# Chunked attention and a two-layer MLP: q and k transposed by VectorE in 32x32 blocks from the tenth group on

## Chip, cores and metric

The kernel runs on one core of a Trainium2 chip. The metric is the device time of one execution in microseconds (us). The engines are TensorE (PE in the profile; PEld is its weight load), VectorE (DVE), ScalarE (ACT), GpSimd (POOL, which also issues the loads) and SyncE (SP, which issues the stores).

## What is computed

```python
batch, n_heads, seq, head_dim = (8, 8, 576, 64)          # q, k, v, float32
# attention inside chunks of 64 positions
scores = (1 / sqrt(64)) * q_c @ k_c.T                     # per batch, head and chunk: 64 x 64
attn = exp(scores - max(scores)); attn = attn / (sum(attn) + 1e-9)
out = attn @ v_c
x = out.transpose(0, 2, 1, 3).reshape(4608, 512)          # tokens x (heads * head_dim)
# the MLP: d_model 512, d_ff 2048
h = x @ w_in
result = maximum(0.01 * h, h) @ w_out                     # 4608 x 512, float32
```

## The kernel before

All matrix work is in float16 with float32 sums. The 4608 tokens are cut into 36 groups of 128 tokens (two chunks of 64 positions); a batch of 576 tokens is 4.5 groups, so every second batch begins in the middle of a group. A group goes through a chain of stages, which the main loop interleaves: iteration `it` works on group `it` (transposes), `it - 1` (scores, softmax) and `it - 2` (attention output).

- `load_qk(u)` (L79): GpSimd issues one DMA for q and one for k of group u, with tokens on the partitions (128 tokens x 8 heads x 64), converted to float16 on the way; two DMAs each where the group straddles two batches. There are `NIN` = 9 buffers per tensor, and loads run five iterations ahead.
- `stage_t(u)`: eight TensorE transposes (L216 into `qp`, L218 into `kp`, with `ident`) put the head dimension on the partitions, two heads at a time. VectorE copies `qp` into the tile `QZ` in two halves of 64 partitions (L221), each into its own place between zeros; ScalarE copies `kp` to `KT` (L223).
- `stage_s(u)`: eight matmuls QZ x KT give the scores `Sp` of 8 heads and 2 chunks (L230). VectorE takes the maximum `mx` (L234) and subtracts it into `sh` (L236).
- `stage_x(u)`: ScalarE's exponential `ex` (L242).
- `stage_n(u)`: VectorE's sum `z` (L247), `ze`, reciprocal `zi`, and the product `en` (L253).
- `stage_e(u)`: four TensorE transposes of `en` into `tpe` (L261); VectorE copies them to `et` (L263).
- `stage_v(u)`: eight matmuls of `VB` (v of the batch) and `et` into `xp` (L272); ScalarE copies it to `xT` (L281), after which the group's 128 tokens may be used by the MLP. When a batch's last chunk is done, `load_v` (L92) issues the v of the batch after next into the same buffer, so its two DMAs wait on GpSimd's queue for those matmuls, and the q and k loads issued after them wait behind them.

The MLP is cut into 288 chunks of equal TensorE work. `mm1` (L151, 144 chunks) makes `hT` from `xT` and `w_inT`, and ScalarE takes the leaky relu into `gT` (L158). `mm2` (L167, 144 chunks, four to an output tile) makes `oP` from `gT` and `w_outT`; ScalarE copies a finished tile to `osb` (L176) and SyncE stores it. `fill(n)` issues the next n chunks of a fixed list, or stops when their tokens aren't there yet. Token blocks of the MLP are 128 (eight), 256 (two) and 512 (six) long.

Every engine executes its instructions in the order written. From iteration 5 on TensorE's order is: S of group it-1, `fill(2)`, E of it-2, T of it, `fill(2)`, V of it-2, `fill(2)`; VectorE's is mx, sh, et, the two copies to QZ, z, ze, zi, en. After the last group the chunks that are left are issued in one go.

Of the kernel before, what the change touches and what calls it, by code (L numbers as in the profile page):

```python
# [8 lines left out]
FP16 = mybir.dt.float16  # L9
# [7 lines left out]
def kernel(  # L17
# [21 lines left out]
    nc = tc.nc  # L39

    B, H, S, D = q.shape
# [3 lines left out]
    CH = 64  # L45
# [3 lines left out]
    SCL = float(D) ** -0.5  # L49
    NQZ = 3  # L50
    NVB = 2
    NIN = 9
    G = 2 * CH

    NU = n_tok // G
    BLOCKS = [128] * 8 + [256] * 2 + [512] * 6

    sbp = ctx.enter_context(tc.tile_pool(name="k_sb", bufs=1))
# [5 lines left out]
    QZ = [sbp.tile([128, 4, 2, 2, CH], FP16, name=f"QZ{i}") for i in range(NQZ)]  # L64
# [5 lines left out]
    def load_qk(u):  # L70

        both = []
        for name, src in (("q_in", q), ("k_in", k)):
            t = sbp.tile([128, H, D], FP16, name=name, tag=name, bufs=NIN)
            r0, r1 = u * G, (u + 1) * G
            cut = min(-(-r0 // S) * S, r1) if r0 % S else r1
            for a, z in ((r0, cut), (cut, r1)):
                if a < z:
                    nc.gpsimd.dma_start(  # L79
                        out=t[a - r0:z - r0],  # L80
                        in_=src[a // S, :, a % S:a % S + z - a, :].rearrange("h p d -> p h d"),
                    )
            both.append(t)
        qk[u] = tuple(both)

    def zero_vb(i, eng):
        for m in range(2):
            eng.memset(VB[i][m * CH:(m + 1) * CH, :, :, (1 - m) * CH:(2 - m) * CH], 0.0)

    def load_v(b):  # L90
        for m in range(2):
            nc.gpsimd.dma_start(  # L92
                out=VB[b % NVB][m * CH:(m + 1) * CH, :, :, m * CH:(m + 1) * CH].rearrange("p h c d -> p (h c) d"),
                in_=v[b, m * H // 2:(m + 1) * H // 2].rearrange("h (c j) d -> j (h c) d", j=CH),
            )
# [8 lines left out]
    def load_w_out(f0, f1):  # L104
# [3 lines left out]
        )  # L108

    load_qk(0)  # L110
    ident = sbp.tile([128, 128], FP16, name="ident")
    make_identity(nc, ident)
# [28 lines left out]
    def mm1(j, a):  # L141
        tb, r0 = BLOCKS[j], START[j]
        nf = 512 // tb
        if a == 0:
            tag, bufs, pad = ("gS", 4, 128) if tb == 128 else ("gT", 2, 512)
            gT[j] = sbp.tile([128, NFC, tb], FP16, name="gT", tag=tag, bufs=bufs, padded_shape=[128, NFC, pad])
        hT = psp.tile([128, nf, tb], FP32, name="hT", tag="mm", bufs=4)
        for i in range(nf):
            fc = nf * a + i
            for t in range(NT):  # L150
                nc.tensor.matmul(  # L151
                    out=hT[:, i, :],
                    lhsT=w_inT[:, t, fc * 128:(fc + 1) * 128],
                    rhs=xT[:, t, r0:r0 + tb],
                    start=(t == 0),
                    stop=(t == NT - 1),
                )
        nc.scalar.activation(  # L158
            out=gT[j][:, nf * a:nf * a + nf, :], in_=hT, func=AFT.Prelu, bias=0.0, scale=1.0, alpha=0.01
        )  # L160

    def mm2(j, ti, part):
        if part == 0:
            oP[j, ti] = psp.tile([128, d_model], FP32, name="oP", tag="mm", bufs=4)
        o = oP[j, ti]
        for fc in range(part * 4, part * 4 + 4):
            nc.tensor.matmul(  # L167
                out=o,
                lhsT=gT[j][:, fc, ti * 128:(ti + 1) * 128],
                rhs=w_outT[:, fc, :],  # L170
                start=(fc == 0),
                stop=(fc == NFC - 1),
            )
        if part == NFC // 4 - 1:
            osb = sbp.tile([128, d_model], FP32, name="osb", tag="osb", bufs=3)
            nc.scalar.activation(out=osb, in_=o, func=AFT.Copy, bias=0.0, scale=1.0)  # L176
            r0 = START[j] + ti * 128
            nc.sync.dma_start(out=out[r0:r0 + 128, :], in_=osb)
# [12 lines left out]
    def fill(n):  # L191
        for _ in range(n):
            if state["pos"] == len(chunks):
                return
            kind, j, a, p = chunks[state["pos"]]
            if START[j] + BLOCKS[j] > state["tokens"]:
                return
            state["pos"] += 1
            if kind == "mm1":
                mm1(j, a)  # L200
            else:
                mm2(j, a, p)
# [8 lines left out]
    def stage_t(u):  # L211
# [10 lines left out]
        KT[u] = sbp.tile([128, 4, 2, CH], FP16, name="KT", tag="KT", bufs=2)  # L222
        nc.scalar.activation(out=KT[u], in_=kp, func=AFT.Copy, bias=0.0, scale=1.0)  # L223

    def stage_s(u):
        qz, kt = QZ[u % NQZ], KT.pop(u)
        Sp = psp.tile([128, 8, CH], FP32, name="Sp", tag="Sp", bufs=1)
        for i in range(8):
            g, e, m = i // 4, i // 2 % 2, i % 2
            nc.tensor.matmul(  # L230
                out=Sp[:, i, :], lhsT=qz[:, 2 * m + g, e, :, :], rhs=kt[:, 2 * m + g, e, :], start=True, stop=True
            )
        mx = sbp.tile([128, 8], FP32, name="mx", tag="mx", bufs=2)
        nc.vector.tensor_reduce(out=mx, in_=Sp, axis=AXL.X, op=ALU.max)  # L234
        SH[u] = sbp.tile([128, 8, CH], FP32, name="sh", tag="sh", bufs=2)
        nc.vector.tensor_tensor(  # L236
            out=SH[u], in0=Sp, in1=mx.unsqueeze(2).to_broadcast((128, 8, CH)), op=ALU.subtract
        )

    def stage_x(u):  # L240
        E[u] = sbp.tile([128, 8, CH], FP16, name="ex", tag="ex", bufs=2)
        nc.scalar.activation(out=E[u], in_=SH.pop(u), func=AFT.Exp, bias=0.0, scale=SCL)  # L242

    def stage_n(u):
        ex = E.pop(u)
        z = sbp.tile([128, 8], FP32, name="z", tag="z", bufs=2)
        nc.vector.tensor_reduce(out=z, in_=ex, axis=AXL.X, op=ALU.add)  # L247
        ze = sbp.tile([128, 8], FP32, name="ze", tag="ze", bufs=2)
        nc.vector.tensor_scalar_add(out=ze, in0=z, scalar1=1e-9)
        zi = sbp.tile([128, 8], FP32, name="zi", tag="zi", bufs=2)  # L250
        nc.vector.reciprocal(out=zi, in_=ze)
        E[u] = sbp.tile([128, 8, CH], FP16, name="en", tag="en", bufs=2)
        nc.vector.tensor_tensor(  # L253
            out=E[u], in0=ex, in1=zi.unsqueeze(2).to_broadcast((128, 8, CH)), op=ALU.mult
        )

    def stage_e(u):
        en = E.pop(u)
        tpe = psp.tile([128, 4, 128], FP16, name="tpe", tag="ox", bufs=1)
        for i in range(4):  # L260
            nc.tensor.transpose(out=tpe[:, i, :], in_=en[:, 2 * i:2 * i + 2, :], identity=ident)  # L261
        et = sbp.tile([128, 2, 2, 2, CH], FP16, name="et", tag="et", bufs=2)
        nc.vector.tensor_copy(out=et, in_=tpe)  # L263
        ET[u] = et

    def stage_v(u):
        et = ET.pop(u)
        xp = psp.tile([128, NT, 2, CH], FP32, name="xp", tag="ox", bufs=1)
        for e in range(2):
            b, c = divmod(2 * u + e, NCH)  # L270
            for t in range(NT):
                nc.tensor.matmul(  # L272
                    out=xp[:, t, e, :],
                    lhsT=VB[b % NVB][:, t, c, :],
                    rhs=et[:, t // 2, e, t % 2, :],
                    start=True,
                    stop=True,
                )
            if c == NCH - 1 and b + NVB < B:
                load_v(b + NVB)  # L280
        nc.scalar.activation(out=xT[:, :, u * G:(u + 1) * G], in_=xp, func=AFT.Copy, bias=0.0, scale=1.0)  # L281
        state["tokens"] = (u + 1) * G


    for it in range(NU + 2):
        if it < 5:
            if it >= 2:
                stage_e(it - 2)
            if it >= 1:
                stage_s(it - 1)  # L290
            if it >= 2:
                stage_v(it - 2)
            if it >= 1:
                stage_x(it - 1)
            fill(2)
            if it >= 1:
                stage_n(it - 1)
            stage_t(it)
            if it > 2:
                fill(2)  # L300
        else:
            if it <= NU:
                stage_s(it - 1)
            fill(2)
            if it <= NU:
                stage_x(it - 1)
            stage_e(it - 2)
            if it < NU:
                stage_t(it)
            if it <= NU:  # L310
                stage_n(it - 1)
            fill(2)
            stage_v(it - 2)
            fill(2)
        if 0 < it and it + 5 < NU:
            load_qk(it + 5)
    fill(len(chunks))


# [28 lines left out]
```

## Time and profile before

| | us |
|---|---|
| median of 3 runs | 323.13 (322.86 to 324.0) |
| span of the profiled execution, first to last instruction | 322.2 |
| TensorE busy | 300.4 |
| ScalarE busy | 165.4 |
| VectorE busy | 161.5 |
| GpSimd busy, mostly issuing loads | 98.3 |

The page of the profile gives a span for the profiled execution and no other time of it; the times of the runs are of other executions. Busy shares are means over the span: the attention stages end at about 246 us, and from there on only the MLP is left.

### The profile page before, as it was taken

The page shows a single profiled execution, that of the slowest core. Times are in us where ns is not written, and L with a number is a line of the kernel's source. Part 1 is how long each engine was busy: PE and PEld are TensorE (multiplying, and loading weights), DVE is VectorE, ACT ScalarE, POOL GpSimd, SP SyncE. Part 2 cuts the span into 40 slices and gives each one's busy share as a digit, 9 for nine tenths or more (in the row PEclk, how much of TensorE's full clock was granted, in tenths as well). Part 3 has the DMA queues.
Part 4 walks back from the last instruction along what each step waited for, and adds up shares of the span by engine and source line. Part 5 has one row for each costly group of instructions (what it writes and reads, how often), then busy time and mean ns, then how long its engine had stood idle before and what let it go on. Part 6 is the DMA issues. An engine that isn't in the chain of part 4 may idle for free.

```text
span 322.2 us, 6197 instructions
## 1 busy us (share of the span) xinstructions
PE 300.4 (93%) x2608; PEld 182.8 (57%) x2608; DVE 161.5 (50%) x330; ACT 165.4 (51%) x290; POOL 98.3 (31%) x116
## 2 busy tenths in 40 slices
PE   2477789999999999999999999999999999999995
PEld 1367685578778677555555555555554444444442
DVE  5755757666766675777667667756760000000000
ACT  2244644456665565586348734883477137316611
POOL 8763997505800560490057036000000000000000
PEclk9997979999999999999999999999999999999999
DMA  9999999955990695499169429600100020020011
GB/s 69 175 193 187 182 154 149 196 68 67 174 99 33 46 181 45 88 154 66 65 72 167 33 41 184 79 2 36 65 34 2 35 96 2 2 96 35 0 65 65
DMA packets 121627, 28.18 MB, mean 87 GB/s; under 512 B 112896, under 2 KB 116992, under 8 KB 121600
## 3 DMA queue, kind: packets, MB, share of 16 engines
q0 software_dynamic: 116416, 18.36, 77.1%
q1 hardware_dynamic: 5184, 9.44, 7.9%
q8 instruction: 20, 0.33, 0.4%
q14 instruction: 7, 0.06, 0.0%
HBM read 36.70 MB, written 9.44 MB: 143 GB/s over the span
## 4 chain that ended last, share of the span: by engine, by line
PE 86%; DMA 9%; POOL 3%; issue 1%; ACT 1%; ACTq 0%; POOLq 0%
PE oP L167 39%; PE hT L151 36%; DMA w_outT<-in_moe_w_out_dram 4%; DMA k_in<-in_k_dram 3%; DMA w_inT<-in_moe_w_in_dram 3%; PE xp L272 2%; PE Sp L230 2%; PE tpe L261 2%; PE kp L218 2%; PE qp L216 2%; POOL k_in L79 1%; POOL VB L92 1%; POOL w_inT L99 1%; POOL q_in L79 0%; POOL w_outT L105 0%
## 5 line engine op out<-in xcount | busy, mean ns | idle before, releaser
L151 PE MATMUL hT<-xT,w_inT 128*128 128x128 f16 (+2 forms) x1024 | 139.0, 293 | 4.7 <-DMA w_inT<-in_moe_w_in_dram 3.0
L167 PE MATMUL oP<-w_outT,gT 128*128 128x512 f16 x576 | 132.7, 379 | 0.0
L158 ACT ACTIVATE gT<-hT 128x512 f16<-128x512 f32 x144 | 85.8, 597 | 42.9 <-PE hT L151 42.7
L151 PEld LDWEIGHTS <-w_inT 128*128 128x128 f16 x1024 | 80.9, 102 | 44.8 <-issue 5.2
L167 PEld LDWEIGHTS <-gT 128*128 128x128 f16 x576 | 53.4, 98 | 56.7
L176 ACT ACTIVATE osb<-oP 128x512 f32<-128x512 f32 x36 | 21.5, 597 | 75.0 <-PE oP L167 69.2
L234 DVE TENSOR_REDUCE mx<-Sp 128x8 f32<-128x512 f32 x36 | 24.9, 692 | 44.5 <-PE Sp L230 44.5
L92 POOL DMA_DIRECT2D VB<-in_v_dram x16 | 18.5, 1160 | 85.9 <-PE xp L272 85.9
L79 POOL DMA_DIRECT2D k_in<-in_k_dram x40 | 35.3, 882 | 7.2 <-DMA w_inT<-in_moe_w_in_dram 2.5
L79 POOL DMA_DIRECT2D q_in<-in_q_dram x40 | 35.3, 889 | 4.7 <-DMA w_outT<-in_moe_w_out_dram 1.8
L221 DVE COPY QZ<-qp 64x512 f16<-64x512 f16 x72 | 30.1, 418 | 5.1 <-PE qp L216 4.6
L242 ACT ACTIVATE ex<-sh 128x512 f16<-128x512 f32 x36 | 22.5, 624 | 11.6 <-DVE sh L236 11.6
L281 ACT ACTIVATE xT<-xp 128x512 f16<-128x512 f32 x36 | 21.4, 593 | 11.7 <-PE xp L272 11.7
L223 ACT ACTIVATE KT<-kp 128x512 f16<-128x512 f16 x36 | 21.3, 592 | 11.6 <-PE kp L218 11.6
L247 DVE TENSOR_REDUCE z<-ex 128x8 f32<-128x512 f16 x36 | 24.7, 686 | 4.4 <-ACT ex L242 3.4
L263 DVE COPY et<-tpe 128x512 f16<-128x512 f16 x36 | 15.3, 425 | 22.4 <-PE tpe L261 22.4
L253 DVE TENSOR_TENSOR en<-ex,zi 128x512 f16<-128x512 f16 x36 | 24.9, 691 | 1.2
L236 DVE TENSOR_TENSOR sh<-Sp,mx 128x512 f32<-128x512 f32 x36 | 24.9, 691 | 1.2
L216 PE MATMUL qp<-ident,q_in 128*128 128x128 f16 x144 | 14.9, 229 | 8.7 <-DMA q_in<-in_q_dram 8.7
L230 PEld LDWEIGHTS <-QZ 128*128 128x128 f16 x288 | 13.6, 100 | 9.1 <-DVE QZ L221 1.5
L272 PEld LDWEIGHTS <-VB 128*128 128x128 f16 x288 | 13.2, 99 | 6.6 <-issue 0.4
L230 PE MATMUL Sp<-KT,QZ 128*128 128x64 f16 x288 | 14.8, 196 | 2.2 <-ACT KT L223 1.3
(22 smaller groups left out, 108.9 us busy)
## 6 DMA issues: line engine op xcount, KB each, us to landing
out_dram<-osb SPq DMA_DIRECT2D x36, 256.0 KB, 2.0
VB<-in_v_dram POOLq DMA_DIRECT2D x16, 288.0 KB, 5.7
q_in<-in_q_dram POOLq DMA_DIRECT2D x32, 128.0 KB, 6.0
k_in<-in_k_dram POOLq DMA_DIRECT2D x32, 128.0 KB, 5.9
w_inT<-in_moe_w_in_dram POOLq DMA_DIRECT2D x8, 256.0 KB, 8.5
w_outT<-in_moe_w_out_dram POOLq DMA_DIRECT2D x4, 512.0 KB, 11.1
q_in<-in_q_dram POOLq DMA_DIRECT2D x8, 64.0 KB, 6.7
k_in<-in_k_dram POOLq DMA_DIRECT2D x8, 64.0 KB, 6.2
```

The lines of the kernel that those rows point to most:

```text
L79: nc.gpsimd.dma_start(out=t[a - r0:z - r0], in_=src[a // S, :, a % S:a % S + z - a, :].rearrange("h p d -> p h d"),)
L92: nc.gpsimd.dma_start(out=VB[b % NVB][m * CH:(m + 1) * CH, :, :, m * CH:(m + 1) * CH].rearrange("p h c d -> p (h c) d"), in_=v[b, m * H // ...
L151: nc.tensor.matmul(out=hT[:, i, :], lhsT=w_inT[:, t, fc * 128:(fc + 1) * 128], rhs=xT[:, t, r0:r0 + tb], start=(t == 0), stop=(t == NT - 1),)
L158: nc.scalar.activation(out=gT[j][:, nf * a:nf * a + nf, :], in_=hT, func=AFT.Prelu, bias=0.0, scale=1.0, alpha=0.01)
L167: nc.tensor.matmul(out=o, lhsT=gT[j][:, fc, ti * 128:(ti + 1) * 128], rhs=w_outT[:, fc, :], start=(fc == 0), stop=(fc == NFC - 1),)
L221: nc.vector.tensor_copy(out=qz[s * CH:(s + 1) * CH, :, :, s, :], in_=qp[s * CH:(s + 1) * CH])
L230: nc.tensor.matmul(out=Sp[:, i, :], lhsT=qz[:, 2 * m + g, e, :, :], rhs=kt[:, 2 * m + g, e, :], start=True, stop=True)
L234: nc.vector.tensor_reduce(out=mx, in_=Sp, axis=AXL.X, op=ALU.max)
L236: nc.vector.tensor_tensor(out=SH[u], in0=Sp, in1=mx.unsqueeze(2).to_broadcast((128, 8, CH)), op=ALU.subtract)
L242: nc.scalar.activation(out=E[u], in_=SH.pop(u), func=AFT.Exp, bias=0.0, scale=SCL)
L247: nc.vector.tensor_reduce(out=z, in_=ex, axis=AXL.X, op=ALU.add)
L253: nc.vector.tensor_tensor(out=E[u], in0=ex, in1=zi.unsqueeze(2).to_broadcast((128, 8, CH)), op=ALU.mult)
```

## The change

Groups 0 to 8 (batches 0 and 1) stay as they are. From group `UD` = 9 on:

- q and k come per batch, by `load_qk_batch(b)`, with 16 DMAs of GpSimd per batch: for each tensor, each half `m` of the heads, each pair of heads `s` and each half `dh` of the head dimension, one DMA to 32 partitions. A partition holds one position inside blocks of 32 positions; what is contiguous is 32 numbers of the head dimension (128 bytes read, 64 written). The tiles `q_d` and `k_d` have three buffers each. Batch b is issued at the end of iteration 9b // 2 - 5 (4, 8, 13, 17, 22, 26 for batches 2 to 7).
- VectorE's `transpose` turns each 32x32 block and writes QZ (`stage_dq`, two halves of 64 partitions x 512 elements) and KT (`stage_dk`, 128 x 512). A group that straddles two batches (13, 22 and 31) has each of them in two pieces, by `cuts`.
- The eight TensorE transposes and the three copies of `stage_t` are gone for these groups. VectorE's order becomes mx, sh, first half of q, et, second half of q, k, z, ze, zi, en.
- The heads pair up differently on the partitions, so `stage_v` reads `et` in another order.
- The last `fill(2)` of an iteration becomes `fill(3)` while such groups are prepared (iterations 9 to 35).
- `load_qk` ends with group 8, and its buffers go from 9 to 6.

```diff
-    NIN = 9
+    NIN = 6
+    UD = 9
...
+    def load_qk_batch(b):
+        both = []
+        for name, src in (("q_d", q), ("k_d", k)):
+            t = sbp.tile([128, 2, 2, S // 32, 32], FP16, name=name, tag=name, bufs=3)
+            for m in range(2):
+                for s in range(2):
+                    for dh in range(2):
+                        p0 = s * 64 + dh * 32
+                        h0 = 4 * m + 2 * s
+                        nc.gpsimd.dma_start(
+                            out=t[p0:p0 + 32, m, :, :, :].rearrange("p h b d -> p (h b) d"),
+                            in_=src[b, h0:h0 + 2, :, dh * 32:dh * 32 + 32].rearrange("h (b t) d -> t (h b) d", t=32),
+                        )
+            both.append(t.rearrange("p m h b d -> p (m h) (b d)"))
+        qkd[b] = tuple(both)
...
+    def cuts(u):
+        r0, r1 = u * G, (u + 1) * G
+        cut = min(-(-r0 // S) * S, r1) if r0 % S else r1
+        return [(a // S, a % S, (a - r0) // CH, (z - a) // CH) for a, z in ((r0, cut), (cut, r1)) if a < z]
+
+    def stage_dq(u, s):
+        qz = QZ[u % NQZ]
+        for b, at, e0, n in cuts(u):
+            nc.vector.transpose(
+                out=qz[s * CH:(s + 1) * CH, :, e0:e0 + n, s, :],
+                in_=qkd[b][0][s * CH:(s + 1) * CH, :, at:at + n * CH].rearrange("p h (e t) -> p h e t", e=n),
+            )
+
+    def stage_dk(u):
+        KT[u] = sbp.tile([128, 4, 2, CH], FP16, name="KT", tag="KT", bufs=2)
+        for b, at, e0, n in cuts(u):
+            nc.vector.transpose(
+                out=KT[u][:, :, e0:e0 + n, :],
+                in_=qkd[b][1][:, :, at:at + n * CH].rearrange("p h (e t) -> p h e t", e=n),
+            )
...
-                    rhs=et[:, t // 2, e, t % 2, :],
+                    rhs=et[:, t // 2, e, t % 2, :] if u < UD else et[:, t % 2, e, t // 2, :],
...
+            dve = UD <= it < NU
             if it <= NU:
                 stage_s(it - 1)
+            if dve:
+                stage_dq(it, 0)
             fill(2)
             if it <= NU:
                 stage_x(it - 1)
             stage_e(it - 2)
-            if it < NU:
+            if dve:
+                stage_dq(it, 1)
+                stage_dk(it)
+            elif it < UD:
                 stage_t(it)
             if it <= NU:
                 stage_n(it - 1)
             fill(2)
             stage_v(it - 2)
-            fill(2)
-        if 0 < it and it + 5 < NU:
+            fill(3 if dve else 2)
+        if 0 < it and it + 5 < UD:
             load_qk(it + 5)
+        for b in range(2, B):
+            if it == 9 * b // 2 - 5:
+                load_qk_batch(b)
```

More of the change, by code (lines that the diff above doesn't have):

```diff
@@ L84, in load_qk @@
         qk[u] = tuple(both)
+    qkd: dict[int, tuple[bass.AP, bass.AP]] = {}
+    def load_qk_batch(b):
[13 more added lines that the diff above has]
+        qkd[b] = tuple(both)
     def zero_vb(i, eng):
```

## The prediction

> **What bounds the kernel now.** I read the page's busy times and slices first, then one long window, then the chain of waits over two iterations, and then the rows of the engines that receive work.
>
> ```profile
> span 322.2 us, 6197 instructions
> ...
> PE 300.4 (93%) x2608; PEld 182.8 (57%) x2608; DVE 161.5 (50%) x330; ACT 165.4 (51%) x290; POOL 98.3 (31%) x116
> ...
> PE   2477789999999999999999999999999999999995
> ...
> DVE  5755757666766675777667667756760000000000
> ...
> DMA  9999999955990695499169429600100020020011
> GB/s 69 175 193 187 182 154 149 196 68 67 174 99 33 46 181 45 88 154 66 65 72 167 33 41 184 79 2 36 65 34 2 35 96 2 2 96 35 0 65 65
> ...
> 44.00:304.00 260.00, 260.00 (x2201) 153.05 (x2200) 133.97 (x278) 144.88 (x256) 65.02 (x74) 1.00 0.78 77
> ```
>
> The slices (8.06 us each) show TensorE with holes only at the start, where DMA is full. The last line is the stage from 44 to 304 us: TensorE is busy in 260.00 of 260.00 us at granted clock 1.00, VectorE in 133.97, ScalarE in 144.88, GpSimd in 65.02. A busy TensorE could still hide waits, so the chain of waits must say what it does:
>
> ```profile
> 103.26 0.23 PE Sp L230 x8
> 103.49 1.75 PE hT L151 x16
> 105.24 0.22 PE tpe L261 x4
> 105.46 0.22 PE qp L216 x4
> 105.68 0.22 PE kp L218 x4
> 105.91 1.75 PE hT L151 x16
> 107.65 0.23 PE xp L272 x8
> 107.89 1.73 PE oP L167 x8
> 109.61 0.23 PE Sp L230 x8
> ```
>
> This is one iteration, 103.26 to 109.61: 6.35 us, all of it TensorE, piece behind piece. The two fill chunks between stages cost 1.73 to 1.75, 0.87 each. The eight transposes that the change takes out stand at 105.46 and 105.68, 0.22 + 0.22 = 0.44 us. Nothing in the chain waits for VectorE, ScalarE or a load.
>
> **The change, part by part.**
>
> *Removed from TensorE.* Groups 9 to 35 are 27 groups; each loses 0.44 us: 27 x 0.44 = 11.9 us. This is the whole expected gain. Its price is a pitch, not a duration:
>
> ```profile
> L216 PE MATMUL qp<-ident,q_in x144: 216/219/314, 4.9 to 231.9; 128*128 128x128 f16 x144
> ```
>
> One transpose lasts 219 ns, but four end 0.22 us after they began to be the chain, 55 ns each. The Trainium skill (TensorE: Matmul & The Clock Gate, Part 4: PE-mode transpose) gives about 275 ns for one in a kernel; taken as a cost, that would be 59 us for 216. The trace disagrees with that use: the row has 219 ns and the chain 55.
>
> *The seventh chunk.* `fill(3)` in place of `fill(2)` moves chunks from behind the last group to between stages; the total stays 288. By the order of chunks and tokens, each call from iteration 6 on finds its chunk ready, with seven per iteration too (233 issued after iteration 37 instead of 206, 55 left instead of 82). It is worth nothing by itself; it lengthens an iteration to 6.35 - 0.44 + 0.87 = 6.78 us, which gives VectorE more room.
>
> *ScalarE* loses the copy to KT, 27 x 0.59 (page row L223: mean 592). It is not on the chain, so I count nothing.
>
> ```profile
> L223 ACT ACTIVATE KT<-kp 128x512 f16<-128x512 f16 x36 | 21.3, 592 | 11.6 <-PE kp L218 11.6
> ```
>
> *VectorE.* It loses two copies and gets three block transposes. Its iteration before:
>
> ```profile
> 109.88 0.69 DVE L234 TENSOR_REDUCE mx<-Sp 128x8 f32<-128x512 f32 x1 [1.31 <-PE Sp L230]
> 110.61 0.69 DVE L236 TENSOR_TENSOR sh<-Sp,mx 128x512 f32<-128x512 f32 x1
> 111.83 0.42 DVE L263 COPY et<-tpe 128x512 f16<-128x512 f16 x1 [0.53 <-PE tpe L261]
> 112.17 0.85 DVE L221 COPY QZ<-qp 64x512 f16<-64x512 f16 x2
> 113.05 0.69 DVE L247 TENSOR_REDUCE z<-ex 128x8 f32<-128x512 f16 x1
> 113.77 0.17 DVE L249 TENSOR_SCALAR ze<-z 128x8 f32<-128x8 f32 x1
> 113.98 0.20 DVE L251 RECIPROCAL zi<-ze 128x8 f32<-128x8 f32 x1
> 114.22 0.69 DVE L253 TENSOR_TENSOR en<-ex,zi 128x512 f16<-128x512 f16 x1
> ```
>
> Without the QZ copies, by starts: 0.73 (mx) + 0.72 (sh) + 0.43 (et) + 0.72 (z) + 0.21 + 0.24 + 0.72 (en) = 3.77 us. The trace has no transpose on VectorE. The rows with 512 elements per partition lie between 0.42 (the copies) and 0.69 (reduce, subtract, multiply). I take 0.70, since a transpose that passes one element at a time is nearest to the rows of 0.69; as ends I keep 0.42 and 1.38, two passes of a 0.69 row. With 0.70: 3.77 + 3 x 0.70 = 5.9 us of 6.78. In groups 13, 22 and 31, which straddle two batches, each transpose splits in two; 0.69 against 0.17 for an almost empty instruction puts the extra at about 0.17 each, so 6.4 us. Still inside.
>
> Order matters as much, because VectorE is in order. From the start of S (109.61): sh ends at +1.69; the first q transpose fills +1.72 to +2.42; et, ready at +2.22 before, now runs +2.42 to +2.87. V on TensorE comes at 0.23 + 1.74 + 0.22 + 1.74 = +3.93, so the wait is covered by 1.06 us. The other two transposes end at about +4.3, the next S needs them at +6.78 (2.5 us of cover); z to en end at about +6.2, and en is needed at +8.75. VectorE is free 0.85 us before the next Sp arrives. If the cover of et goes, V waits; if that of dk goes, S waits.
>
> *Loads.* Before, a group loads 2 tensors of 1024 rows of 64 numbers; after, a batch comes in 2 x 8 DMAs of 32 x 36 = 1152 pieces of 32 numbers, 18432 packets of half the size for 4.5 groups, where 9216 stood before.
>
> ```profile
> 43.93 0.94 POOL L79 DMA_DIRECT2D k_in<-in_k_dram  x1
> 44.80 0.96 POOL L79 DMA_DIRECT2D q_in<-in_q_dram  x1
> ...
> 50.66 2.31 POOL L92 DMA_DIRECT2D VB<-in_v_dram  x2 [2.28 <-PE xp L272]
> ...
> q0 software_dynamic: 116416, 18.36, 77.1%
> q1 hardware_dynamic: 5184, 9.44, 7.9%
> ...
> DMA packets 121627, 28.18 MB, mean 87 GB/s; under 512 B 112896, under 2 KB 116992, under 8 KB 121600
> ...
> 80.50:86.00 5.50, 5.50 (x90) 4.68 (x87) 4.03 (x8) 3.41 (x6) 5.50 (x8) 1.00 2.39 158
> ...
> 58.36 0.40 PE L230 MATMUL Sp<-KT,QZ 128*128 128x64 f16 x8
> ...
> 64.67 0.40 PE L230 MATMUL Sp<-KT,QZ 128*128 128x64 f16 x8
> ```
>
> GpSimd's queue: one q or k DMA takes 0.87 us (43.93 to 44.80) for 1024 packets, one V DMA 1.16 for 2304, so about 0.90 for 1152, 14.4 us per batch. The DMA engines: 158 GB/s of 128 B packets is 1.23 packets per ns, 15.0 us per batch if a packet of half the bytes costs the same. In the slices with weights, whose rows are eight times longer, the rate is 182 to 193 GB/s, only a fifth more, so most of a packet's cost goes with its bytes, and the ratio r of a new packet to an old one should lie between 0.6 and 1. I take 1. Per batch V adds 4608 packets (3.8 us), and the output 4.5 x 0.079 x 322.2 / 36 = 3.2 us: 22 of the 30.5 us that 4.5 iterations last. Sustained, it fits until r = 1.56.
>
> The narrow place is the first batch. It is issued behind group 8, at 44.80, to 59.2. The DMA engines have by my estimate of the backlog (at 1.23 packets per ns) worked off the earlier loads at about 49, so it lands at 49 + 15 + 2 = 66. Iteration 9 starts its S at 64.67 (GpSimd's 50.66 is released by V of iteration 6; three S later). q is wanted at 66.4 and is first in the queue; k at 68, with 2.5 us more before S(9) waits: 70.7. That holds until r = 1.3. V of batch 2, behind it on GpSimd's queue, moves from 50.66 to 59.2 and is wanted by V(9) near 82; batch 3 follows by 76, wanted near 94. Behind later V loads, which wait for TensorE on the same queue, batches come some 40 us ahead of use. Three buffers per tensor: batch 5 takes the place of batch 2, which group 13 released three iterations earlier. I count loads at nothing, covered by 4.7 us at the first batch.
>
> The Trainium skill (DMA: Bandwidth & Descriptors, Specifications) speaks against this part: below 512 B a DMA engine does a read-modify-write, so smaller pieces would not get cheaper. The row agrees that such packets are the rule here, 112896 of 121627 are under 512 B; if their price were all per packet, r would be 1, and the sum would stay as it is.
>
> *Sum:* 322.2 - 11.9 = 310.3 us of span. The page gives no other time of that execution; the median of the runs is 323.13, 0.9 above its span, and I keep that: 311.2 us.
>
> **Rivals.**
>
> *VectorE becomes the bound (slower).* Place: between mx and en in each iteration. It starts to cost when three transposes exceed 6.78 - 3.77 = 3.01 us, 1.00 each, and eats the gain when 27 x (3.77 + 3X - 6.78) = 11.9, X = 1.15. At 1.38 each: 27 x 1.13 = 30.5, so 342 us. For it: 87% to 94% of the iteration (5.9 to 6.4 of 6.78 us) is spoken for, and the price is not in the trace. Against: no row of 512 elements exceeds 0.69. Chance 0.09, of which 0.06 above X = 1.15.
>
> *Loads become the bound (slower).* If the small packets cost r = 2, a batch with V and output takes 37 us against 30.5; the sixth lands at about 49 + 6 x 37 - 5 = 266 instead of the 220 at which group 31 wants it, 46 us late: 357 us. It eats the gain from about r = 1.6. Against: weight rows and small rows differ little per byte. Chance 0.06.
>
> *Only the first batches are late.* r from 1.3 to 1.6, or GpSimd slower than 1.49 us per DMA: (70.7 - 2 - 44.8) / 16. At r = 1.5 batch 2 is 3 us late and batch 3 about 5: 314 to 317 us. Chance 0.08.
>
> *The change gives nothing:* the freed TensorE time turns idle, 323 us. Against: every piece of the chain from 44 us on is TensorE. Chance 0.03.
>
> *A transpose costs its duration:* 216 x 0.219 = 47 us, 276. Against: the chain's starts. Chance below 0.01. The skill's 275 ns, above, would make it 264.
>
> **How the numbers follow.** The forecast, all added work covered, has 0.74: 311.2, its own range 310 to 313 for leftovers of up to 0.07 us per iteration. Forecast 0.74, late first batches 0.08 and a VectorE just over its room 0.02 make faster 0.84; nothing gained 0.03 and a VectorE near 1.15 0.01 make same 0.04; VectorE 0.06 and loads 0.06 make slower 0.12. (0.5% is what a measurement can tell.) The range goes from 309.8 to 317, up to the late batches.
>
> **What would show it.** Right: no qp or kp in the chain after about 60 us, pieces tpe and hT or oP adjoining, 6.8 us from Sp to Sp, TensorE busy in all of a stage like 70 to 290; transposes of about 0.7 us; q_d and k_d landing ahead of group 9's use. Wrong: a wait of Sp for QZ or KT, or of xp for et, that recurs in each iteration (VectorE), or VectorE's transposes waiting for q_d or k_d at iterations 9, 13, 18 (loads); DMA full slices up to 220 us with less than 75 GB/s would mean r near 2.

## The result and the profile after

| us | before | changed |
|---|---|---|
| median of the runs | 323.53 (322.86 to 324.0, 4 runs) | 311.44 (310.71 to 311.64, 4 runs) |
| span of the profiled execution | 322.2 | 308.9 |
| its own time | not listed | 310.71 |

The ratio is 0.9623, 95% interval 0.9597 to 0.9649: 12.1 us less. The forecast was 311.2, the range 309.8 to 317.

From the page of the changed kernel:

```profile
span 308.9 us, 5832 instructions
...
PE 285.6 (92%) x2392; PEld 167.7 (54%) x2392; DVE 194.6 (63%) x366; ACT 152.8 (49%) x263; POOL 125.4 (41%) x152
...
q0 software_dynamic: 172288, 18.36, 135.7%
```

The stage from 44 to 290 us in one window (length, busy time and count of TensorE, its weight loads, VectorE, ScalarE and GpSimd, granted clock, DMA share, GB/s):

```profile
44.00:290.00 246.00, 246.00 (x1975) 139.41 (x1972) 165.93 (x314) 131.59 (x228) 92.47 (x110) 1.00 1.54 82
```

TensorE is still busy in all 246 us. It has 216 fewer matmuls (2392 instead of 2608), VectorE 33 us more to do (194.6 instead of 161.5). The chain of waits over one iteration:

```profile
104.59 0.23 PE Sp L270 x8
104.82 1.73 PE oP L186 x8
106.55 0.22 PE tpe L301 x4
106.77 1.73 PE oP L186 x8
108.50 0.23 PE xp L312 x8
108.73 1.73 PE oP L186 x8
110.46 0.87 PE hT L170 x8
111.33 0.23 PE Sp L270 x8
```

It lasts 6.74 us, piece behind piece: no qp and no kp, seven chunks instead of six, nothing but TensorE. VectorE in one iteration:

```profile
77.61 0.69 DVE L274 TENSOR_REDUCE mx<-Sp 128x8 f32<-128x512 f32 x1 [0.91 <-PE Sp L270]
78.33 0.69 DVE L276 TENSOR_TENSOR sh<-Sp,mx 128x512 f32<-128x512 f32 x1
78.94 0.69 DVE L252 STREAM_TRANSPOSE QZ<-q_d 64x512 f16<-64x512 f16 x1
79.57 0.41 DVE L303 COPY et<-tpe 128x512 f16<-128x512 f16 x1
80.01 0.71 DVE L252 STREAM_TRANSPOSE QZ<-q_d 64x512 f16<-64x512 f16 x1
80.75 0.71 DVE L260 STREAM_TRANSPOSE KT<-k_d 128x512 f16<-128x512 f16 x1
81.39 0.64 DVE L287 TENSOR_REDUCE z<-ex 128x8 f32<-128x512 f16 x1
82.07 0.17 DVE L289 TENSOR_SCALAR ze<-z 128x8 f32<-128x8 f32 x1
82.27 0.20 DVE L291 RECIPROCAL zi<-ze 128x8 f32<-128x8 f32 x1
82.51 0.69 DVE L293 TENSOR_TENSOR en<-ex,zi 128x512 f16<-128x512 f16 x1
```

A transpose takes 0.69 to 0.71 us, and VectorE still waits 0.91 us for these scores (1.14 in most later iterations). The first loads per batch on GpSimd's queue:

```profile
45.16 6.71 POOL L98 DMA_DIRECT2D q_d<-in_q_dram  x8
51.86 0.81 POOL L98 DMA_DIRECT2D k_d<-in_k_dram  x1
52.88 5.64 POOL L98 DMA_DIRECT2D k_d<-in_k_dram  x7 [0.21 <-issue]
```

The eight of them that bring k, from issue to landing:

```profile
DMA to landing us min/median/max: 6.4/7.1/7.7
```

VectorE's first uses, from its timeline:

```profile
65.23 0.69 DVE L252 STREAM_TRANSPOSE QZ<-q_d 64x512 f16<-64x512 f16 x1
...
67.11 0.71 DVE L260 STREAM_TRANSPOSE KT<-k_d 128x512 f16<-128x512 f16 x1
```

The last k load is issued by 57.7 and lands by 65.4 at the latest. VectorE takes k at 67.11 and doesn't wait for it.

The two profiled spans differ by 13.3 us, more than the times. The rest lies before the change begins: in the profiled execution of before, TensorE's clock was down just ahead of the stage in question. In both profiles TensorE has then waited 1.00 us for `xT`; the same 32 matmuls behind that wait, before and in the changed kernel:

```profile
42.34 3.49 PE L151 MATMUL hT<-xT,w_inT 128*128 128x128 f16 x32 [1.00 <-ACT xT L281]
42.67 1.95 PE L170 MATMUL hT<-xT,w_inT 128*128 128x128 f16 x32 [1.00 <-ACT xT L321]
```

The window from 44 to 46 us, before:

```profile
44.00:46.00 2.00, 2.00 (x28) 2.00 (x27) 0.00 (x0) 0.73 (x2) 2.00 (x4) 0.60 2.44 162
```

and in the changed kernel:

```profile
44.00:46.00 2.00, 2.00 (x44) 2.00 (x41) 1.08 (x2) 1.17 (x3) 2.00 (x4) 1.00 2.41 154
```

S of iteration 9 starts at 64.67 before and at 63.47 in the changed kernel, 1.2 us earlier, though nothing that the change touches has run on TensorE by then. It varies from execution to execution: in later runs of the kernel before, those with a mean clock of 0.989 have spans of 322.0 to 323.9, those with 0.999 or more 320.2 to 321.5. The medians, not the two profiles, give the change's worth.

### The profile page after: what moved, and what is told of

Its sections match the earlier page's. It is cut to its first block, busy times and chain, and to the rows that moved or that the text cites. A ratio compares the mean times of both kernels' runs of the same rounds, so it can differ in the third digit from the quotient of the medians.

```text
span 308.9 us, 5832 instructions
## 1 busy us (share of the span) xinstructions
PE 285.6 (92%) x2392; PEld 167.7 (54%) x2392; DVE 194.6 (63%) x366; ACT 152.8 (49%) x263; POOL 125.4 (41%) x152
## 3 DMA queue, kind: packets, MB, share of 16 engines
q0 software_dynamic: 172288, 18.36, 135.7%
## 4 chain that ended last, share of the span: by engine, by line
PE 85%; DMA 9%; POOL 3%; issue 1%; ACT 1%; ACTq 0%; POOLq 0%
PE oP L186 40%; PE hT L170 37%; DMA w_outT<-in_moe_w_out_dram 4%; DMA w_inT<-in_moe_w_in_dram 3%; DMA k_in<-in_k_dram 3%; PE xp L312 2%; PE Sp L270 2%; PE tpe L301 2%; POOL k_in L80 1%; POOL VB L111 1%; POOL w_inT L118 1%; POOL q_in L80 0%; PE kp L237 0%; POOL w_outT L124 0%; PE qp L235 0%
## 5 line engine op out<-in xcount | busy, mean ns | idle before, releaser
L170 PE MATMUL hT<-xT,w_inT 128*128 128x128 f16 (+2 forms) x1024 | 137.2, 289 | 4.6 <-DMA w_inT<-in_moe_w_in_dram 3.0
L170 PEld LDWEIGHTS <-w_inT 128*128 128x128 f16 x1024 | 78.7, 99 | 45.5 <-issue 5.2
L98 POOL DMA_DIRECT2D k_d<-in_k_dram x48 | 38.8, 813 | 5.4 <-DMA q_d<-in_q_dram 3.7
L98 POOL DMA_DIRECT2D q_d<-in_q_dram x48 | 38.9, 829 | 2.9 <-DMA VB<-in_v_dram 2.7
L252 DVE STREAM_TRANSPOSE QZ<-q_d 64x512 f16<-64x512 f16 (+1 forms) x60 | 38.2, 644 | 0.8
L282 ACT ACTIVATE ex<-sh 128x512 f16<-128x512 f32 x36 | 22.5, 625 | 13.5 <-DVE sh L276 13.3
L287 DVE TENSOR_REDUCE z<-ex 128x8 f32<-128x512 f16 x36 | 23.6, 655 | 3.0 <-ACT ex L282 2.9
L260 DVE STREAM_TRANSPOSE KT<-k_d 128x512 f16<-128x512 f16 (+1 forms) x30 | 19.4, 654 | 0.8
L270 PEld LDWEIGHTS <-QZ 128*128 128x128 f16 x288 | 13.5, 100 | 9.1 <-DVE QZ L240 1.5
L312 PE MATMUL xp<-et,VB 128*128 128x64 f16 x288 | 14.5, 194 | 0.3 <-DVE et L303 0.3
```

The costliest lines, as they stand in the source:

```text
L98: nc.gpsimd.dma_start(out=t[p0:p0 + 32, m, :, :, :].rearrange("p h b d -> p (h b) d"), in_=src[b, h0:h0 + 2, :, dh * 32:dh * 32 + 32].rear ...
L170: nc.tensor.matmul(out=hT[:, i, :], lhsT=w_inT[:, t, fc * 128:(fc + 1) * 128], rhs=xT[:, t, r0:r0 + tb], start=(t == 0), stop=(t == NT - 1),)
L252: nc.vector.transpose(out=qz[s * CH:(s + 1) * CH, :, e0:e0 + n, s, :], in_=qkd[b][0][s * CH:(s + 1) * CH, :, at:at + n * CH].rearrange("p ...
L270: nc.tensor.matmul(out=Sp[:, i, :], lhsT=qz[:, 2 * m + g, e, :, :], rhs=kt[:, 2 * m + g, e, :], start=True, stop=True)
L312: nc.tensor.matmul(out=xp[:, t, e, :], lhsT=VB[b % NVB][:, t, c, :], rhs=et[:, t // 2, e, t % 2, :] if u < UD else et[:, t % 2, e, t // 2, :],
```

## The experiments

Three series shared chips and runs of the kernel before, with medians of 322.97, 322.71 and 322.49. Beside their ratios to it, I compare the new kernels with 311.44. The changed kernel itself ran beside the kernel before at 323.53, so a cost found in this way is up to 1 us smaller than the same cost by the ratios.

**Eight TensorE transposes put back.**

```diff
                 stage_dk(it)
+                stage_pe_again()      # 8 transposes of ident into qp and kp
```

> The changed kernel with eight TensorE transposes per group put back from the tenth group on (of the identity, into qp and kp, read by nobody), where the old ones stood in TensorE's order. Everything else stays as changed. Theory A (the gain is TensorE time, 55 ns a transpose, 0.44 us a group): 27 x 0.44 = 11.9 us are lost again, 323.3 us, ratio to the kernel before 0.998 to 1.002. Rival B (the gain came from the seventh chunk, from ScalarE's relief or from the start of the execution): clearly under 320 us.

Measured: 322.98, ratio 1.0003 (0.9976 to 1.003). The whole gain is gone, with VectorE's transposes, the loads per batch, the seventh chunk and ScalarE's relief all still in place. Its chain of waits:

```profile
107.63 1.73 PE oP L186 x8
109.36 0.22 PE tpe L308 x4
109.58 0.22 PE qp L270 x4
109.80 0.22 PE kp L270 x4
110.03 1.73 PE oP L186 x8
```

The same 0.44 us stand in the chain again. Theory A holds, B falls.

**The sixth chunk only.**

```diff
-            fill(3 if dve else 2)
+            fill(2)
```

> The changed kernel with fill(2) at the end of every iteration again, so an iteration has six chunks and lasts 5.9 us instead of 6.75. Theory A (the seventh chunk is only moved): same time, 311.4 within 0.6 us, with VectorE at 5.65 of 5.9 us just inside its room (measured by starts, mx to the end of en) and at about 6.0 of 5.9 in the three split groups. Rival B (the seventh chunk is part of the gain, because VectorE needs its room): VectorE becomes the bound, some 0.2 us or more per iteration, 316 us or more.

Measured: 310.88 (310.61 to 311.16), ratio 0.9613 (0.9581 to 0.9645): the same. The seventh chunk only moves work.

**One ScalarE copy put back.**

```diff
                 stage_dk(it)
+                nc.scalar.activation(out=xtra, in_=w_inT[:, 0, 0:512], func=AFT.Copy, bias=0.0, scale=1.0)
```

> The changed kernel with one ScalarE copy of 128x512 per group put back (of a weight slice into a tile that nobody reads), behind the transposes of VectorE. Theory A (ScalarE is off the path): same, 311.4 within 0.6 us. Rival B (part of the gain is ScalarE's relief): up to 27 x 0.59 = 16 us slower.

Measured: 310.66 (310.14 to 311.07), ratio 0.9605 (0.9572 to 0.9638). The same; ScalarE's relief was worth nothing.

**One, two and three more VectorE transposes per group.**

```diff
                 stage_dk(it)
+                for _ in range(1):    # 2 and 3 in the other two kernels
+                    nc.vector.transpose(out=xtra, in_=w_inT[:, 0, 0:512])
```

> The changed kernel with one more VectorE transpose of 128x512 per group (of a weight slice into a tile that nobody reads), behind the one of k: 0.74 us by starts. Theory A: VectorE goes from 5.65 to 6.4 of 6.75 us, still covered: 311.4 within 0.6 us. Rival B (VectorE's order already delays TensorE, 0.74 us per group on the path): 27 x 0.74 = 20 us slower, 331 us.

> The changed kernel with two more VectorE transposes of 128x512 per group (of a weight slice into a tile that nobody reads), behind the one of k. Theory A: VectorE needs 5.65 + 2 x 0.74 = 7.13 us in an iteration of 6.75, so it becomes the bound by some 0.4 us per group, 27 x 0.4 = 11 us: 322 us (318 to 326), and the trace shows TensorE waiting. Rival B (VectorE's slack is larger than by starts, because waits between its instructions shrink): under 315 us.

> The changed kernel with three more VectorE transposes of 128x512 per group (of a weight slice into a tile that nobody reads). In the run with two more, VectorE ran without a gap at 6.80 us from group to group, so without the extra ones it needs 6.80 - 1.34 = 5.46, not the 5.87 of the prediction, and one more transpose adds 0.67. Theory A (VectorE's need is 5.46 + 0.67 per extra transpose, and TensorE's 6.75 hides it up to there): 7.47 us per group, 27 x 0.72 = 19.4 us, and 0.5 for the split groups: 331 us (329 to 333). Rival B (the 6.80 of the last run was set by something else than VectorE, such as the chunks): under 320 us.

Measured: 310.88 with one (ratio 0.961, 0.9572 to 0.9647), 313.41 with two (0.9702, 0.9651 to 0.9753), 333.0 with three (1.0323, 1.029 to 1.0356). One is free. Two cost 2.0 us instead of the 11 that I expected: theory A falls there, and rival B holds. VectorE's timeline with two more, from one mx to the next, with the two extra transposes between:

```profile
222.63 0.68 DVE L275 TENSOR_REDUCE mx<-Sp 128x8 f32<-128x512 f32 x1
226.36 1.42 DVE L356 STREAM_TRANSPOSE xtra<-w_inT 128x512 f16<-128x512 f16 x2
229.43 0.68 DVE L275 TENSOR_REDUCE mx<-Sp 128x8 f32<-128x512 f32 x1
```

With three more:

```profile
202.38 0.68 DVE L275 TENSOR_REDUCE mx<-Sp 128x8 f32<-128x512 f32 x1
209.93 0.68 DVE L275 TENSOR_REDUCE mx<-Sp 128x8 f32<-128x512 f32 x1
```

and TensorE's timeline there:

```profile
202.52 0.40 PE L302 MATMUL tpe<-ident,en 128*128 128x128 f16 x4 [0.36 <-DVE en L294]
```

None of the mx rows has a wait in brackets any more: VectorE runs without a gap, 6.80 us from group to group with two more, 7.55 with three. The two take 1.34 us (226.36 to 227.70, where z begins), so VectorE needs about 5.46 without them. With two more, the three groups that straddle two batches take 6.97, only 0.17 more, and five groups take 7.07 to 7.23: in these, ze lasts 0.41 to 0.60 us instead of 0.17, while GpSimd issues loads (see the last section). The third adds 0.75, not the 0.67 of my expectation; 27 x (7.55 - 6.74) = 21.9 us on 311.44 gives 333.3, close to the time measured. So the bound passes to VectorE between mx and en, as the prediction said that it could, only later. What TensorE waits for is mostly en, which its E reads (25 waits of 10.0 us in all with three more), and hardly et (three of 0.5 us in all); the extra transposes stand behind k, ahead of z and en, so that et is delayed only by way of the next iteration.

**The first batch eight and sixteen loads later.**

```diff
+        ahead = (("q_x", q),) if b == 2 else ()        # and ("k_x", k) in the second kernel
-        for name, src in (("q_d", q), ("k_d", k)):
+        for name, src in (*ahead, ("q_d", q), ("k_d", k)):
```

> The changed kernel with eight more loads ahead of the first batch's sixteen (q of that batch into a tile that nobody reads), so that the whole first batch comes 8 x 0.84 = 6.7 us later. Theory A (the first batch has a cover of some 5 us for k: last load issued at 57.7, landed at about 65, wanted by S(9) at 70.3): k lands at about 71.7, S(9) waits about 2 us: 313.5 us (312 to 316). Rival B (loads are far from any limit): 311.4. Rival C (loads already cost the changed kernel time): 6.7 us slower, 318.

> As the run with eight more loads, with sixteen (q and k of that batch into tiles that nobody reads): 13.5 us later. Theory A: 13.5 minus a cover of about 4.5 us, so 9 us slower: 320.5 us (318 to 322). Rival B (far from any limit): 311.4 to 313.

Measured: 313.83 (312.95 to 315.13; ratio 0.9714, 0.967 to 0.9757) and 321.77 (320.91 to 323.92; 0.9958, 0.9928 to 0.9988): 2.4 and 10.3 us later than 311.44, against 2 and 9 expected. VectorE's and then TensorE's timeline with eight more:

```profile
71.38 0.71 DVE L261 STREAM_TRANSPOSE KT<-k_d 128x512 f16<-128x512 f16 x1 [4.62 <-DMA VB<-in_v_dram]
```

```profile
72.14 0.39 PE L271 MATMUL Sp<-KT,QZ 128*128 128x64 f16 x8 [1.97 <-DVE KT L261]
```

VectorE's with sixteen more, then TensorE's, then the window from 72 to 76 us:

```profile
70.13 0.70 DVE L253 STREAM_TRANSPOSE QZ<-q_d 64x512 f16<-64x512 f16 x1 [4.58 <-DMA q_d<-in_q_dram]
```

```profile
71.19 0.39 PE L313 MATMUL xp<-et,VB 128*128 128x64 f16 x8 [3.30 <-DVE et L304]
79.69 0.59 PE L271 MATMUL Sp<-KT,QZ 128*128 128x64 f16 x8 [3.83 <-DVE KT L261]
```

```profile
72.00:76.00 4.00, 3.86 (x11) 1.28 (x10) 0.63 (x1) 0.22 (x1) 4.00 (x5) 0.60 5.62 85
```

With eight more, VectorE waits for k (the profile names a load of V, which came last by its records; what the instruction reads is k_d), and TensorE's S waits behind it for 1.97 us. With sixteen, et too is late, because VectorE stands before the first half of q with et behind it in its queue. About 0.7 us of each wait of S is VectorE's own transpose. Behind the waits the granted clock is lower, 0.60 in that window, so that a late load costs somewhat more than the wait: 2.4 us for 1.97 of waiting, 10.3 for 7.13. In the result's two profiles the clock fell after a wait of 1.00 us in one and not in the other; when it falls was not tested. Only the first batch makes TensorE wait.

**Pieces of 16 numbers instead of 32.**

```diff
-                    for dh in range(2):
+                    for dq in range(4):
+                        dh, x = dq // 2, dq % 2
...
-                            out=t[p0:p0 + 32, m, :, :, :].rearrange(...)
-                            in_=src[b, h0:h0 + 2, :, dh * 32:dh * 32 + 32].rearrange(...)
+                            out=t[p0:p0 + 32, m, :, :, x * 16:x * 16 + 16].rearrange(...)
+                            in_=src[b, h0:h0 + 2, :, dq * 16:dq * 16 + 16].rearrange(...)
```

> The changed kernel with each load cut again: pieces of 16 numbers (64 bytes read, 32 written), 32 loads per batch instead of 16. Theory A (GpSimd's 0.84 us per load is the limit of the loads, packets of any size follow): 27 us + 2.3 of V per batch against 30.3 us that 4.5 iterations last; the first batch lands near 78.6 instead of 70.2 and the second near 108 instead of 97: some 11 us slower, 322 us. Rival B (the DMA engines pay per packet, about 0.7 ns per packet over all 16, and the loads become the bound): 36864 packets take 25 to 27 us plus 7 of V and output, 2 to 4 us more per batch than 30.3: 330 us or more. Rival C (the DMA engines pay by bytes and GpSimd by rows): under 316.

Measured: 316.89 (315.97 to 318.76), ratio 0.9812 (0.9765 to 0.986): 5.5 us slower than the changed kernel, half of A's 11. GpSimd's timeline:

```profile
57.89 12.87 POOL L99 DMA_DIRECT2D k_d<-in_k_dram  x16
```

All its k loads from issue to landing, VectorE's and TensorE's timeline where they wait, and the page's row of the queue:

```profile
DMA to landing us min/median/max: 2.7/3.6/5.4
```

```profile
73.20 0.71 DVE L261 STREAM_TRANSPOSE KT<-k_d 128x512 f16<-128x512 f16 x1 [6.45 <-DMA k_d<-in_k_dram]
73.97 0.39 PE L271 MATMUL Sp<-KT,QZ 128*128 128x64 f16 x8 [3.80 <-DVE KT L261]
```

```profile
q0 software_dynamic: 284416, 18.37, 200.6%
```

GpSimd's 0.81 us per load is the limit, as A says: sixteen loads in 12.87 us without a pause. Those of the first batch's k land 3.8 us after their issue in the median, where the eight of the changed kernel took 7.1. I had added the old landing time, which held a queue in it, so k is there at 73.20, 5 us earlier than the 78.6 that I said. No later batch held TensorE up: VectorE waited once more, 0.99 us at 101.23 for the next batch's k, and TensorE did not. B falls: the DMA engines did 1152 packets in 0.81 us, 1.42 per ns, load after load, and were not the limit; batch 3 was begun 28.2 us after batch 2 (73.01 and 44.82), within the 30.3 that it had. Why the packets of 32 bytes don't queue and those of 64 do was not followed up.

**The change from group 18 on.**

```diff
-    UD = 9
+    UD = 18
...
-        for b in range(2, B):
+        for b in range(4, B):
```

> The change from the nineteenth group on (UD = 18, loads per batch from batch 4 on) instead of the tenth: 18 groups instead of 27. Theory A (each group gives its 0.44 us of TensorE time): 18 x 0.44 = 7.9 us, 315.1 us, ratio to the kernel before 0.974 to 0.977. Rival B (the gain has a fixed part, from the start of the execution, where the loads of the first groups change): the same 311.4 or close to it; or, if the early batch loads cost something, less than 315.

Measured: 314.83 (314.09 to 315.93), ratio 0.9764 (0.9723 to 0.9805), 7.7 us under its 322.49. Eighteen groups give 7.7 us, 27 give 12.1: 0.43 and 0.45 us per group. No fixed part shows, though the scatter of the runs would hide one of about 1 us, and the early batches cost nothing that can be told. No version here beats the changed kernel by more than the measurement can tell.

## Why the prediction was right

- *The gain is TensorE's pitch, 27 x 0.44 = 11.9 us.* Shown three ways: 12.1 measured, all of it lost when eight transposes come back (1.0003), and in proportion to the groups (7.7 for 18). The run with the eight put back is the strongest of the three, since it leaves every other part of the change in place. That 311.2 and 311.44 agree to 0.2 us is in part luck: the kernel before has medians from 322.49 to 323.53 in its four sets of runs. Taking the duration instead (0.219 each) would have said 276 us.
- *The seventh chunk and ScalarE are worth nothing.* Shown by the runs that undo each: 310.88 and 310.66.
- *A VectorE transpose costs 0.70.* Measured 0.69 to 0.71, at the rows of 0.69 that I took; the far end of 1.38 wasn't needed. Why it takes as long as those rows was not tested.
- *VectorE needs 5.9 us per group.* This term was too large: 5.46 when it runs without a gap. In the run with `fill(2)`, too, an iteration lasts only 5.87 us (Sp at 152.18 and 158.05), and TensorE waits for nothing. I had added the starts of the old order, where nearly every instruction waited for the one before it. In the new order neighbours with nothing to do with each other overlap by some 0.07 us. The prediction's own rows held one such case that the sum passed over: et at 111.83 lasts 0.42, and the copy to QZ begins 0.34 after it, where I counted 0.43. In the changed kernel the first half of q starts 0.61 us after sh, which lasts 0.69, et 0.63 after that, z 0.64 after k. The second half of q starts only when et has ended, and k when that has. The Trainium skill (VectorE: DVE Perf Modes, Two Vector instructions with no wait between them) states such a rule, that an instruction is held until all earlier ones have finished when its operands start in another quarter of the partitions than the last ones did; the second half of q starts at partition 64, k at 0 again, and the rows agree. The extra for a straddling group was too large as well: 0.17 us in the run with two more, where I had 0.17 for each of three transposes.
- *The VectorE rival begins at 1.00 us per transpose and eats the gain at 1.15.* Both came too early by the same 0.4 us per group: with 5.46 measured, the room is 1.28 us, so it begins near 1.13 and eats the gain near 1.28. That VectorE's work becomes the bound is shown, 333.0 us with three more. It shows with extra transposes behind k, though: TensorE then waits mostly for en, and not for et, QZ or KT as my signs of being wrong had it. Transposes that last longer themselves, which would also delay et, were not tried.
- *The first batch lands at 66 and has until 70.7.* Measured 65.4 at the latest, in an execution that ran 1.2 us ahead; there S of group 9 starts at 70.32, so k had until about 69.6, a cover of 4.2 us where I had said 4.7. The two delayed runs agree: VectorE takes k at 71.38 and 78.92, 6.0 and 13.5 us later than 65.4, and S of group 9 starts at 72.14 and 79.69, 1.8 and 9.4 later than 70.32, so 4.2 and 4.1 us were covered. The 0.6 and 0.9 us that are left of 2.4 and 10.3 come after that start, where the granted clock is lower: 0.57 from 72 to 76 us with eight more, 0.57 from 78 to 86 with sixteen.
- *r lies between 0.6 and 1.* Not measured by itself; the landing at 65.4, near the 66 that r = 1 gave, has the estimate of the backlog in it too. That packets of 32 bytes went through at 1.42 per ns, against 1.23 per ns of 128 bytes, excludes only that these cost more. GpSimd's time, estimated at 0.90, was 0.81.
- *The execution's own time.* I set the median 0.9 us above the span. In the changed profile the time is 310.71 for a span of 308.9, 1.8 more, and the profiled execution of before was one with a lowered clock, some 1.2 us slow. Neither error reaches the forecast: the span less 11.9 plus 0.9 is the median of 323.13 less 11.9.

## What to carry to other kernels

When one engine fills the chain of waits without a gap, what leaves that engine is gained at its pitch in the chain, as long as each thing added elsewhere has a cover larger than its price; the list of covers, with the rows they come from, is the prediction. An engine in order can have more room than the sum of its old start-to-start times when the new neighbours don't depend on each other, as here 5.46 us of work where the sum said 5.9; adding copies of one of its instructions until it runs without a gap measures that room, here with the second copy. And of these loads, issued far ahead, only the first batch was narrow: look for the time at which it can be issued and the time at which its reader stands in its queue.

## What the runs showed of the hardware

The share of a DMA queue in the page does not say how full the DMA engines are. It went from 77.1% to 135.7% and 200.6% of the time of sixteen engines while no batch after the first made TensorE wait; with 32-byte pieces the loads even landed sooner, q 5.3 and k 3.6 us after issue in the median instead of 7.1 and 6.5.

A small VectorE instruction can last longer beside work on GpSimd. In the changed kernel, the addition that makes `ze` from `z`, 8 elements, usually lasts 0.17 us. Once it lasted 2.61, beside the issue of a load and two fills of VB on GpSimd:

```profile
33.07 2.61 DVE L289 TENSOR_SCALAR ze<-z 128x8 f32<-128x8 f32 x1
32.75 0.87 POOL L80 DMA_DIRECT2D k_in<-in_k_dram  x1 [1.69 <-DMA w_outT<-in_moe_w_out_dram]
33.61 4.10 POOL L107 MEMSET VB<- 64x2304 f16 x2
```

In the kernel before it was 1.51, beside the same fills:

```profile
33.81 1.51 DVE L249 TENSOR_SCALAR ze<-z 128x8 f32<-128x8 f32 x1
33.26 4.10 POOL L88 MEMSET VB<- 64x2304 f16 x2
```

Both ended, at 35.68 and 35.32, about when the first of the two fills did (33.61 and 33.26 plus half of 4.10). The Trainium skill (SBUF — State Buffer, Who interferes with whom) says that VectorE and GpSimd share a pair of ports, which one instruction holds to its end, and that instructions of this kind on VectorE can ask for it where their operands meet certain conditions. The rows agree with the end, though no run varied the fills. In the changed kernel ze began 0.54 us before the fill, while the load was still being issued, so a fill alone does not explain that row. From 60 us on, ze lasts 0.26 to 0.83 us in five groups, each time while GpSimd issues a load; others beside such issues last 0.17, as that at 82.07. It cost nothing here; in the run with two more transposes, where VectorE has no room, it is part of what they cost.
